# Small zero products on TensorE ahead of the first y burst of a Mamba-2 scan with a SiLU layer

## The chip, the cores and the metric

The kernel runs on one core of one Trainium2 chip. The metric is the device time of one execution in microseconds (us). Six executions of the kernel before are given by their median. One execution was recorded by the hardware profiler; its span, from the first to the last instruction, is shorter than its time, because the start and the end of the execution lie around it.

## The reference, cut to what matters

A chunked state-space scan over 4 batches, 8 heads, 768 positions, head size 32 and state size 16, and after it a layer with SiLU over the 3072 tokens:

```python
for c in range(nc):                       # chunks of 32 positions
    cum = np.cumsum(la, axis=-1)          # la: log of the decays a
    L = np.exp(cum[..., :, None] - cum[..., None, :]) * causal
    M = np.einsum('bhin,bhjn->bhij', Cc, Bc) * L
    y_intra = np.einsum('bhij,bhjd->bhid', M, xc)
    y_inter = np.einsum('bhin,bhnd->bhid', Cc, state) * np.exp(cum)[..., None]
    y[:, :, sl] = y_intra + y_inter
    state = decay_full * state + sum_j(Bc_j xc_j decay_from_j)
...
h = x @ w_in                              # (3072, 256) @ (256, 2048)
g = h * (1.0 / (1.0 + np.exp(-h)))
out = g @ w_out                           # (3072, 2048) @ (2048, 256)
```

## The kernel before

The 3072 tokens are cut into 12 units of 256 positions, three to a batch. The scan uses chunks of 64 positions, four to a unit. The order of the work on each engine is written out by hand; nothing reorders it.

One unit goes through these steps. f_Ab is a TensorE product that spreads the decays of the unit over the partitions (only for units 0 and 1; the others load them spread out); f_Ek or f_E is a scan on DVE (VectorE) that makes the decay factors E from them. f_T (DVE) or f_TP (TensorE transposes, L349) brings B and C into the layout for products, and f_T2 (ACT, which is ScalarE, L359) splits C by even and odd heads into ce. f_B scales B on POOL (L334, tile BT). f_D0 (L383) is a burst of 32 small TensorE records, the chunk states; f_G0 (L398) a burst of 32, C times B. f_S (DVE, L422 and L424) carries the state from chunk to chunk, f_SM (ACT, L432) splits it, f_M (DVE, L409) multiplies f_G0's result by E. f_Y is the y burst: up to 32 records with the state (L452) and 64 with the masked products (L461). f_X (ACT, L470) copies its result to the tile XM. Then f_s1 (L481) multiplies XM by two column blocks of w_in, eight times for a unit, and SiLU follows on ACT. Later the products with w_out follow (L495, and in another form L572).

The weights come in 16 pieces of 512 KB. w_size (ACT) and w_bits (DVE, then POOL at L182) turn each piece into the form that TensorE uses, and w_bits also issues the load of the piece seven further on (L156, SP's queue). Pieces 0 to 2 are issued in the first microseconds, pieces 3 to 6 after the loads of unit 1, and SP issues the loads of unit 2 after them.

The start of the program is a list in one order: transposes and scan of unit 0, y burst of unit 0, first products of unit 0 between the steps of unit 1, y burst of unit 1, and then a table of f_s1 steps with the steps of unit 2 among them.

`busy(n)` issues n products of zeros on TensorE: the tile `idle` is a row of zeros read as bf16, and the result, written to a PSUM tile of the pool ps_o, is read by nobody. It stands at three places: ahead of f_A and the f_Ab of unit 0 (five products, at the start), between f_G0 and f_D0 of unit 0 (four), and between f_Ab of unit 1 and the y burst of unit 0 (four). On TensorE a product is two instructions, a weight load (PEld) and a matmul (PE).

## Time and profile before

| what | value |
|---|---|
| median of 6 executions | 359.45 us |
| all six | 360.4, 357.52, 359.42, 357.7, 359.66, 359.48 us |
| the profiled execution | 360.4 us, span 358.7 us |
| mean granted clock of TensorE over the span | 0.993 |
| TensorE busy | 346.0 us, 96% of the span |
| DVE, ACT, POOL busy | 51%, 45%, 51% |

In the profile's lists a line begins with the start of a group (us from the span's start) and its length, then engine, line of the code, operation, tiles (out<-in), shape and count; in brackets stands how long the engine was idle before the group, and what released it. "issue" there means that the engine waited for nothing that the profile shows. In a table by stretch the columns are the stretch, its length, the busy time and number of instructions of PE, PEld, DVE, ACT and POOL, then the granted clock of TensorE (1.00 is full), the busy share of the 16 DMA engines and GB/s. In the lists of DMA queues stand packets, MB and the share of 16 engines' time; q1 carries the data that SP issues, q8 and q14 carry instructions.

### The profile page before, as it was taken

To read this page: it belongs to the slowest core of one execution; us is meant where nothing else is said; L and a number is where in the kernel's file an instruction comes from. 1 tells how busy PE (TensorE), PEld (TensorE's weight loads), DVE (VectorE), ACT (ScalarE), POOL (GpSimd) and SP (SyncE) were. 2 spreads that over 40 slices of the span, in tenths; PEclk is the share of its full clock that TensorE was granted. 3 is DMA by queue.
4 is the path that set the end of the run, shared out by engine and by line. 5 is a ranking of instruction groups with operands and counts; after the bars stand their busy time and mean duration, and the time that the engine had idled before them with its cause. 6 is when DMAs were issued, how large, how long until landed. Compare 5 with 4: busy or idle time off the path is not lost.

```text
span 358.7 us, 8309 instructions
## 1 busy us (share of the span) xinstructions
PE 346.0 (96%) x3276; PEld 290.0 (81%) x3277; DVE 183.0 (51%) x389; ACT 160.7 (45%) x390; POOL 181.4 (51%) x246
## 2 busy tenths in 40 slices
PE   7778999999999999999999999999999999999994
PEld 2457888888888888888888888888888888888883
DVE  7977979754267245543455543446542221214722
ACT  2547477223222444645444645444645354454100
POOL 4433335353139168298355298355298930596100
PEclk9998999999999999999999999999999999999999
DMA  6898966761547252162126163110000110001203
GB/s 122 201 333 152 335 177 111 137 116 24 117 87 104 55 96 28 33 117 32 15 53 112 27 107 45 17 17 2 15 2 14 18 16 0 15 2 19 40 2 45
DMA packets 110059, 26.53 MB, mean 74 GB/s; under 512 B 98884, under 2 KB 105796, under 8 KB 110020
## 3 DMA queue, kind: packets, MB, share of 16 engines
q1 hardware_dynamic: 107044, 25.67, 35.3%
q10 hardware_dynamic: 2976, 0.33, 0.6%
q8 instruction: 26, 0.43, 0.5%
q14 instruction: 13, 0.11, 0.1%
HBM read 22.83 MB, written 3.15 MB: 72 GB/s over the span
## 4 chain that ended last, share of the span: by engine, by line
PE 91%; SPq 3%; DMA 2%; issue 1%; ACT 1%; DVE 1%; POOL 0%; ACTq 0%; DVEq 0%
PE o_ps L572 30%; PE hp L655 28%; PE hp L481 15%; PE o_ps L495 8%; PE hp L572 3%; PE gy L461 2%; PE gy L452 2%; PE gy L398 2%; SPq L107 1%; DMA tbc<-in_C_dram 1%; PE gy L383 1%; SPq L156 1%; DMA tbc<-in_B_dram 1%; DMA out_dram<-ot 0%; POOL w_in_sb L182 0%
## 5 line engine op out<-in xcount | busy, mean ns | idle before, releaser
L658 DVE TENSOR_TENSOR gT<-hp,p 128x256 f32<-128x256 f32 x64 | 26.9, 421 | 84.6 <-ACT p L669 47.4
L481 PE MATMUL hp<-XM,w_in_sb 128*128 128x256 f32 x256 | 61.0, 389 | 1.5 <-POOL w_in_sb L182 0.8
L661 ACT ACTIVATE gT<-gT 128x256 f32<-128x256 f32 x96 | 39.7, 413 | 42.8 <-DVE gT L658 42.8
L481 PEld LDWEIGHTS hp<-XM,w_in_sb 128*128 128x128 f32 x256 | 49.1, 194 | 9.7 <-POOL w_in_sb L182 1.7
L572 PE MATMUL o_ps<-gT,w_out_sb 128*128 128x256 f32 x224 | 56.5, 379 | 0.0
L334 POOL TENSOR_TENSOR BT<-bn,E 128x256 f32<-128x256 f32 x12 | 8.6, 717 | 94.7 <-PE hp L655 29.7
L655 PE MATMUL hp<-raw 128*128 128x256 f32 x192 | 52.7, 380 | 0.0
L540 POOL TENSOR_TENSOR gT<-gT 128x256 f32<-128x256 f32 x72 | 51.2, 741 | 0.0
L572 PEld LDWEIGHTS o_ps<-gT,w_out_sb 128*128 128x128 f32 x224 | 42.4, 190 | 5.9
L655 PEld LDWEIGHTS hp<-raw 128*128 128x128 f32 x192 | 36.2, 190 | 5.4 <-POOL ps L543 0.6
L483 ACT ACTIVATE gT<-hp 128x512 f32<-128x512 f32 x32 | 19.1, 596 | 41.2 <-PE hp L481 41.2
L669 ACT ACTIVATE p<-hp 128x256 f32<-128x256 f32 x64 | 24.5, 383 | 27.5 <-PE hp L655 25.7
L658 DVE TENSOR_TENSOR gT<-hp,u 128x256 f32<-128x256 f32 x32 | 13.6, 424 | 40.7 <-PE hp L655 40.7
L655 PE MATMUL hp<-XM,w_in_sb 128*128 128x256 f32 x128 | 34.1, 389 | 0.0
L543 POOL TENSOR_TENSOR ps<-ps 128x256 f32<-128x256 f32 x28 | 20.3, 726 | 26.1 <-ACT ps L579 12.8
L495 PE MATMUL o_ps<-w_out_sb,gT 128*128 128x256 f32 x128 | 30.9, 384 | 0.0
L540 POOL TENSOR_TENSOR TN<-gT 128x256 f32<-128x256 f32 x40 | 28.7, 739 | 0.0
L495 PEld LDWEIGHTS o_ps<-w_out_sb,gT 128*128 128x128 f32 x128 | 23.8, 190 | 3.8 <-issue 0.5
L655 PEld LDWEIGHTS hp<-XM,w_in_sb 128*128 128x128 f32 x128 | 23.3, 190 | 4.3 <-issue 1.0
L297 DVE TENSOR_TENSOR_SCAN E<-ab,diag 128x256 f32<-128x256 f32 (+1 forms) x32 | 24.5, 805 | 3.7 <-PE gy L461 3.3
L540 POOL TENSOR_TENSOR gT<-gT,TN 128x256 f32<-128x256 f32 x32 | 22.1, 730 | 0.0
L579 ACT ACTIVATE ps<-o_ps 128x256 f32<-128x256 f32 x31 | 11.9, 383 | 18.5 <-PE o_ps L572 18.2
(121 smaller groups left out, 542.5 us busy)
## 6 DMA issues: line engine op xcount, KB each, us to landing
ab<-in_a_dram SPq DMA_DIRECT2D x40, 128.0 KB, 3.3
raw<-in_moe_w_in_dram SPq DMA_DIRECT2D x8, 512.0 KB, 7.6
raw<-in_moe_w_out_dram SPq DMA_DIRECT2D x8, 512.0 KB, 6.3
xt<-in_x_dram SPq DMA_DIRECT2D x24, 128.0 KB, 4.0
out_dram<-ot SPq DMA_DIRECT2D x76, 32.0 KB, 1.7
bn<-in_B_dram SPq DMA_DIRECT2D x22, 64.0 KB, 4.9
tbc<-in_C_dram SPq DMA_DIRECT2D x40, 32.0 KB, 2.6
pa<-in_a_dram SPq DMA_DIRECT2D x10, 128.0 KB
```

The source lines that it names most:

```text
L297: nc.vector.tensor_tensor_scan(out=E[u].rearrange("p k h t -> p (k h t)")[:, Q * g0:Q * (g0 + n)], data0=t.rearrange("p g t -> p (g t)"), ...
L481: nc.tensor.matmul(out=hp[:, i], lhsT=w_in_sb[:, kc, f * 128:(f + 1) * 128], rhs=xm[:, kc], start=(kc == 0), stop=(kc == KC - 1))
L483: nc.scalar.activation(GTS[g][:, 2 * j:2 * j + 2], hp, AF.Silu)
L495: nc.tensor.matmul(out=o[:, c], lhsT=GTS[g][:, f, 128 * c:128 * c + 128], rhs=w_out_sb[:, f, :], start=(f == 0), stop=(f == NF - 1), skip_ ...
L540: engine.tensor_tensor(out=o[:, j], in0=a0[:, j], in1=a1[:, j], op=ALU.subtract)
L543: engine.tensor_tensor(out=o, in0=p, in1=q, op=ALU.add)
L572: nc.tensor.matmul(out=o, lhsT=w(j), rhs=g()[:, j], start=(j == 0), stop=(j == NF // 2 - 1))
L579: nc.scalar.activation(pn, on, AF.Copy)
L655: nc.tensor.matmul(out=o, lhsT=w, rhs=x_, start=start, stop=True, skip_group_check=True)
L658: nc.vector.tensor_tensor(out=o, in0=p, in1=q, op=ALU.add)
L661: nc.scalar.activation(o, i, AF.Silu)
L669: nc.scalar.activation(o, i, AF.Copy)
```

## The change

`busy` gets a second count: products of 64 columns with 64 rows of the result, the left operand being 64 columns of zeros. One zero product of 512 columns is taken away at two of the three places, and small ones are put at four: 14 at the start, 24 ahead of f_G0 of unit 0 (a new place), 10 between f_G0 and f_D0, and 30 ahead of the y burst of unit 0. An unused argument goes. No other instruction is touched.

```diff
-    def busy(n, early=True):
-        t = ps_o.tile([128, 512], FP32, name="o_ps") if early else ps_s.tile([128, 4, 512], FP32, name="gy")[:, 0]
+    def busy(n, small=0):
+        t = ps_o.tile([128, 512], FP32, name="o_ps")
         for i in range(n):
             nc.tensor.matmul(out=t, lhsT=idle[:, 0:128], rhs=idle, start=True, stop=True)
+        for i in range(small):
+            nc.tensor.matmul(out=t[:64, :64], lhsT=idle[:, 0:64], rhs=idle[:, 64:128], start=True, stop=True)
...
-    busy(5)
+    busy(4, 14)
     f_A()
...
     f_Ab(0, 0)
     f_Ab(0, 1)
+    busy(0, 24)
     f_G0(0)
-    busy(4)
+    busy(4, 10)
     f_Ek(0, 0)
     f_Ek(0, 1)
     f_B(0)
     f_D0(0, True)
...
     f_Ab(1, 0)
     w_size(1)
-    busy(4)
+    busy(3, 30)
     f_Y(0)
     f_Ab(1, 1)
     f_X(0)
```

## The prediction

> **What bounds the kernel now.** I read the page first, then TensorE's timeline over 32 us, then busy time by stretch, then the DMA queues of short windows. From the page:

> ```profile
> span 358.7 us, 8309 instructions
> ...
> PE 346.0 (96%) x3276; PEld 290.0 (81%) x3277; DVE 183.0 (51%) x389; ACT 160.7 (45%) x390; POOL 181.4 (51%) x246
> ...
> PEclk9998999999999999999999999999999999999999
> ...
> q8 instruction: 26, 0.43, 0.5%
> ```

> TensorE is busy 96% of the span, so a microsecond of its idle time taken away early is a microsecond off the end, if nothing else comes late. The clock row has one slice below 9, the fourth. Queue q8 brings instructions: 26 packets, 0.43 MB, so 16.5 KB each; TensorE's 3276 + 3277 records over 26 packets are 252, so a packet is a block of about 256 TensorE instructions. The timeline of TensorE:

> ```profile
> 7.53 0.70 PE L398 MATMUL gy<-ce,bh 32*64 32x128 f32 x32 [1.03 <-ACT ce L359]
> 8.16 1.04 PE L221 MATMUL o_ps<-gT 128*128 128x512 bf16 x4
> 9.52 0.46 PE L383 MATMUL hp<-xt,BT 64*32 64x64 f32 x32 [0.33 <-POOL BT L334]
> 9.91 1.12 PE L305 MATMUL hp<-gT 108*128 108x512 f32 x2
> 10.87 1.03 PE L221 MATMUL o_ps<-gT 128*128 128x512 bf16 x3
> 13.05 0.58 PE L452 MATMUL gy<-cw,sm 32*64 32x64 f32 x24 [1.15 <-DVE E L409]
> 13.56 0.86 PE L461 MATMUL gy<-E,xt 64*32 64x64 f32 x64
> ...
> 18.12 0.33 PE L349 MATMUL o_ps<-ident,tbc 128*128 128x128 f32 x1 [0.51 <-DMA tbc<-in_C_dram]
> ...
> 27.23 0.34 PE L461 MATMUL gy<-E,xt 64*32 64x64 f32 x15 [1.97 <-issue]
> 28.32 4.31 PE L481 MATMUL hp<-XM,w_in_sb 128*128 128x256 f32 x12 [0.74 <-ACT XM L470]
> ```

> The zero products are L221. The longest gap, 1.97 us, lies inside unit 1's y burst, and its releaser is "issue": no engine held it up. From 28.32 on there is no idle time to the last microseconds. By stretch (TensorE busy first, then its weight loads; the granted clock is the number after POOL):

> ```profile
> 22.74:26.15 3.41, 2.52 (x87) 1.90 (x86) 1.95 (x4) 1.60 (x3) 1.26 (x1) 1.00 1.04 378
> 26.15:29.56 3.41, 1.58 (x21) 1.29 (x21) 0.68 (x2) 1.89 (x4) 0.00 (x0) 1.00 1.06 259
> 29.56:32.97 3.41, 3.41 (x10) 2.66 (x9) 3.32 (x6) 2.69 (x5) 1.44 (x2) 0.50 0.52 105
> ...
> ```

> A stretch with 1.58 of 3.41 us busy is followed by exactly one stretch at half clock: 3.41 us of work took twice its time, so 1.71 us were lost. And the queues from 24.8 to 26 us:

> ```profile
> q1 hardware_dynamic: 230, 0.45, 100.6%
> q8 instruction: 1, 0.02, 5.2%
> ```

> One instruction packet falls in the gap: it starts at 24.91, ends at 25.91, and TensorE goes on at 27.23, 2.32 us after its start. I count 704 instructions (345 + 347 in the stretch 0 to 25.27, and 12 semaphore instructions) before the gap: the edge of a block. Edges one block apart lie after instructions 192, 448, 704, 960. The first three q8 packets start at 14.18, 24.91 and 29.41. So I read it thus: crossing an edge asks for the block after the next. The first edge lies in unit 0's y burst (13.05; packet 1.1 us later, among 64-byte packets), the second in D0 of unit 1 (about 20.2; packet 4.7 us later, behind 2 KB packets of the weight pieces), and that block is what the y burst of unit 1 then lacks.

> **The change, part by part.** It removes two zero products of 512 columns and adds 78 of 64 columns. Each product is two instructions, a weight load and a matmul: 76 x 2 = 152 more, 26 of them ahead of Ab, 74 ahead of G0, 94 ahead of D0, all ahead of unit 0's y burst.

> *Their own time.* No row has a 64-column product by itself. In the records the 512-column ones start 0.215 us apart (0.427 before 5.7 us), an eighth of which is 0.027; the f32 128-column transposes (L349) start 0.107 apart. I take 0.048, half the 97 ns weight load of the wide product, and keep 0.027 and 0.107 as ends.
> First place: -0.43 + 14 x 0.096 at the early clock = +0.9 (0.3 to 2.6). It delays the two Ab products, whose scan on DVE starts at 6.38 after the transposes; the first Ab ended at 5.5, so 0.9 us of cover hides it.
> Second: 24 x 0.048 = 1.15 (0.65 to 2.6) in the 1.03 us for which G0 waits on ScalarE: G0 0.2 late. Its only reader, the mask product (L409), comes at 11.62.
> Third: 10 x 0.048 = 0.48 (0.3 to 1.1) between 9.03 and D0's start at 9.52: D0 0.2 late; DVE reads D0 at 10.49 and it ended at 9.98, 0.5 us of cover.
> Fourth: -0.215 + 30 x 0.048 = 1.2 (0.6 to 3.0) in the 1.15 us before the y burst, which waits for DVE: 0.1 us late.
> On the path +0.1, at most +1.7 at the upper ends (D0 2.2 late less its cover of 0.5; DVE is about 95% busy there and passes it on). Nothing is moved on SP's or POOL's queues, and no other engine waits for a zero product.

> *The edges.* With 94 instructions more, edge 192 lies at the third instruction of D0 of unit 0, crossed near 9.2 us. Edge 448 lies in the y burst of unit 0, at its 124th of 176 instructions, near 14.1. Edge 704 lies at the start of unit 1's y burst. The block needed there is now asked for near 14.1 to 16 us, where the DMA engines are less loaded:

> ```profile
> 8.50:12.90 4.40, 3.02 (x41) 1.08 (x39) 4.18 (x10) 1.48 (x4) 1.41 (x2) 1.00 1.00 328
> ...
> 14.20:17.00 2.80, 2.80 (x33) 1.80 (x17) 2.77 (x5) 1.87 (x4) 2.00 (x3) 1.00 0.40 38
> ```

> With the longest delay seen, 4.7, and 2.32 to use, it is there by 23, a microsecond before unit 1's burst at 23.9. So the 1.97 us gap goes, and with it the idle stretch and its half clock: -1.97 - 1.71 = -3.68. The block after that is asked for near 23.8 and there by 31 at the worst; its first instruction ran at 37.6, less 4.

> *What is late next.* The block needed at 14.1 is now asked for at 9.2, amid the weight pieces (8.5 to 12.9 us, 328 GB/s). Its packet starts 1.1 to 4.7 us later; nearest is the row with the weight pieces, but these end at 12.9, so 13 to 13.9, and the rest of unit 0's y burst runs at 15.3 to 16.2: a new gap of 1.2 to 2.1 us (none at the short delay). I take 1.6, resuming at 15.7. It is mostly covered: TensorE waited 0.51 us at 18.12 for the load of C, and 0.80 us at 21.99 for POOL's w_in_sb. Following TensorE from 15.7: y ends at 16.2, XM at 16.9, s1 18.9, transposes 19.3, s1 20.95, D0 0.85 later than before; the state scan on DVE, which began 0.74 after D0, follows, and unit 1's burst starts at 24.15 instead of 23.92. Cost 0.2; at 16.2 it is 0.7.

> *Whether the gain arrives.* DVE waits 4.12 us to 28.85 for ScalarE, which waits for TensorE's y, so DVE moves with the gap, but not with the half clock. G of unit 2 ran at 47.91 and its BT was done at 45.84: 2.07 us of slack against the 1.7 that TensorE gains on DVE. It holds.

> Sum against the profiled execution's 360.4 (span 358.7): 360.4 - 3.68 + 0.1 + 0.2 = 357.0. The profiled run lies 0.95 above the median of 359.45; from the median, 359.45 - 3.4 = 356.1. Two of the six runs, 357.5 and 357.7, are 1.9 faster than the rest, about the price of one half-clock stretch; I read them as runs without it, and 357.6 - 1.97 + 0.3 = 355.9 agrees.

> [...]
> [...]

> **The rivals.** (a) The new gap falls badly in the clock's stretches: 1.6 plus the wait before y is about 2 us of idle time in 3.4. Then 15.9 to 19.3 runs at half clock, +1.7 not covered: 357.8. For it: 1.83 us sufficed above. Against it: the zero products fill the time before, and two of six runs kept the clock even with the longer gap.
> (b) The change does not do what the edges say: another cause than the block holds the burst at 25.27, and the gap stays: 359.5. Against it: the packet in the gap.
> (c) Slower: the block asked for at 9.2 waits behind all that SP has issued by then, as C's load did, which landed at 18.07. Resuming at 20.4, everything up to unit 1's burst shifts to 29, XM to 31, with a half-clock stretch more: +2.7, so 362.1. It decides from a packet later than about 16 us; the longest delay in the trace, 4.7, gives 13.9.

> **How the numbers follow.** A measurement of this kernel can tell about 0.5%, 1.8 us, from no change: faster is below 357.65, slower above 361.25. Forecast (with or without the covered gap, no half clock) 0.70, of 354.9 to 357.2; (a) 0.13, half of it below 357.65; (b) 0.07; (c) 0.10. The lower end, 354.9, is 357.6 less 1.97 and 0.7 of waits in unit 1's stretch that may shrink; the upper, 359.0, takes in (a) with the small products at their upper price. Faster 0.75, same 0.14, slower 0.11.

> **What would show it.** Right: the first q8 packet starts between 10 and 14 us; unit 1's y burst has no "issue" gap; s1 of unit 1 starts near 26.5, not 28.32, and the stretch after it keeps the full clock; any new "issue" gap lies inside unit 0's burst, before 16.5. Wrong: a gap still at 25 us, D0 of unit 0 later than 10.2, unit 1's burst later than 25, or a clock row below 9 between 16 and 20 us.

## The result, and the profile after

The changed kernel takes 357.44 us (median of 36 executions, 356.36 to 360.4); the kernel before, on the same chips, 359.26 us (78 executions, 357.35 to 362.32). The ratio is 0.9964, with a 95% interval of 0.995 to 0.9979: faster by 0.36%, or 1.3 us, where 3.4 us were forecast. The two medians lie 1.8 us apart; the executions fall into two groups of times, so a median can jump between them, and the means of the table below differ by 1.15 us. The profiled execution of the changed kernel took 356.53 us. The first lines of its page and its clock row:

```profile
span 354.8 us, 8461 instructions
...
PE 346.6 (98%) x3352; PEld 291.7 (82%) x3353; DVE 183.4 (52%) x389; ACT 160.5 (45%) x390; POOL 181.7 (51%) x246
...
PEclk9999999999999999999999999999999999999999
```

Against the page of before the span is 3.9 us shorter with the same busy time, and the slice of the clock row below 9 is gone. TensorE's timeline (L223 is the new small product; all lines below it have moved by two):

```profile
7.09 0.94 PE L223 MATMUL o_ps<-gT 128*64 128x64 bf16 x24
7.97 0.69 PE L400 MATMUL gy<-ce,bh 32*64 32x128 f32 x32
8.59 1.04 PE L221 MATMUL o_ps<-gT 128*128 128x512 bf16 x3
9.56 0.50 PE L223 MATMUL o_ps<-gT 128*64 128x64 bf16 x10
9.99 0.45 PE L385 MATMUL hp<-xt,BT 64*32 64x64 f32 x32
...
12.08 1.14 PE L223 MATMUL o_ps<-gT 128*64 128x64 bf16 x30
13.15 0.58 PE L454 MATMUL gy<-cw,sm 32*64 32x64 f32 x24
13.65 0.64 PE L463 MATMUL gy<-E,xt 64*32 64x64 f32 x38
15.34 0.43 PE L463 MATMUL gy<-E,xt 64*32 64x64 f32 x26 [1.04 <-issue]
...
23.96 0.69 PE L454 MATMUL gy<-cw,sm 32*64 32x64 f32 x32
24.58 0.86 PE L463 MATMUL gy<-E,xt 64*32 64x64 f32 x64
26.13 14.08 PE L483 MATMUL hp<-XM,w_in_sb 128*128 128x256 f32 x64 [0.69 <-ACT XM L472]
```

In before the burst of unit 1 was cut after 49 of its 64 masked products:

```profile
24.54 0.73 PE L461 MATMUL gy<-E,xt 64*32 64x64 f32 x49
27.23 0.34 PE L461 MATMUL gy<-E,xt 64*32 64x64 f32 x15 [1.97 <-issue]
```

In after that 1.97 us gap (24.58) is gone, and s1 of unit 1 starts at 26.13 instead of 28.32. A new "issue" gap of 1.04 us lies in unit 0's burst, after 38 of the 64 records of L463. Ahead of it TensorE's records in the trace number 448 (220 products, 222 weight loads and 6 others), ahead of the gap of before 704: 256 apart, one block by the prediction's count. The first q8 packets start at 12.92 and 21.51 (before: 14.18 and 24.91).

So this one execution did what the prediction said, to half a microsecond (360.4 forecast to become 357.0, and 356.53 measured). Over all executions the gain is little more than a third of what was forecast, so that agreement is in part luck, as the section on the prediction shows.

One sum holds in all fourteen profiles, of before, after and the twelve experiments: the time from the first s1 record of unit 1 to the end of the span, less half of the half-clock time that falls into it, is 328.63 to 328.79 us. (Half clock behind TensorE's last product, in the last microseconds, is not taken off: no product is left to slow down.) All that the change does is decided ahead of that record and by the clock.

The executions also list their mean clock. I call 0.996 and more full clock: what is missing then I put down to the stretch at the very end, which is at half clock in both profiles (from 357.24 us in before, from 354.61 in after). Pooled over four sets of before (104 executions) and two of after (49):

| | full clock: share, mean us | lower clock: share, mean us | mean of all |
|---|---|---|---|
| before | 53 of 104, 358.15 | 51 of 104, 359.94 | 359.03 |
| after | 30 of 49, 357.07 | 19 of 49, 359.16 | 357.88 |

One execution of before, 362.8 us, lies far above the rest; without it the lower-clock mean is 359.88 and the mean of all 358.99. At full clock the change is worth 1.08 us, not the 1.67 net that was forecast for the gap; and the half clock, which was to vanish, is there in 39% of the executions instead of 49%.

### The profile page after: what moved, and what is told of

Same layout as the page of the kernel before. It is cut to its first block, busy times and chain, and to the rows that moved or that the text cites. A ratio compares the mean times of both kernels' runs of the same rounds, so it can differ in the third digit from the quotient of the medians.

```text
span 354.8 us, 8461 instructions
## 1 busy us (share of the span) xinstructions
PE 346.6 (98%) x3352; PEld 291.7 (82%) x3353; DVE 183.4 (52%) x389; ACT 160.5 (45%) x390; POOL 181.7 (51%) x246
## 4 chain that ended last, share of the span: by engine, by line
PE 96%; ACT 1%; DVE 1%; issue 1%; DMA 0%; POOL 0%; SPq 0%; DVEq 0%; ACTq 0%
PE o_ps L574 30%; PE hp L657 28%; PE hp L483 15%; PE o_ps L497 8%; PE hp L574 3%; PE gy L463 3%; PE gy L454 2%; PE gy L400 2%; PE hp L307 1%; PE gy L385 1%; PE o_ps L221 1%; PE o_ps L223 1%; DMA out_dram<-ot 0%; POOL w_in_sb L182 0%; SPq L554 0%
## 5 line engine op out<-in xcount | busy, mean ns | idle before, releaser
L483 PE MATMUL hp<-XM,w_in_sb 128*128 128x256 f32 x256 | 59.3, 381 | 1.0 <-ACT XM L472 0.7
L483 PEld LDWEIGHTS hp<-XM,w_in_sb 128*128 128x128 f32 x256 | 48.1, 190 | 8.5 <-POOL w_in_sb L182 1.1
L657 PE MATMUL hp<-XM,w_in_sb 128*128 128x256 f32 x128 | 34.1, 389 | 0.0
L497 PEld LDWEIGHTS o_ps<-w_out_sb,gT 128*128 128x128 f32 x128 | 23.8, 190 | 3.8 <-issue 0.5
L657 PEld LDWEIGHTS hp<-XM,w_in_sb 128*128 128x128 f32 x128 | 23.3, 190 | 4.3 <-issue 1.0
L581 ACT ACTIVATE ps<-o_ps 128x256 f32<-128x256 f32 x31 | 11.9, 384 | 18.5 <-PE o_ps L574 18.2
```

Of the source, the lines that this page charges most:

```text
L483: nc.tensor.matmul(out=hp[:, i], lhsT=w_in_sb[:, kc, f * 128:(f + 1) * 128], rhs=xm[:, kc], start=(kc == 0), stop=(kc == KC - 1))
L497: nc.tensor.matmul(out=o[:, c], lhsT=GTS[g][:, f, 128 * c:128 * c + 128], rhs=w_out_sb[:, f, :], start=(f == 0), stop=(f == NF - 1), skip_ ...
L581: nc.scalar.activation(pn, on, AF.Copy)
L657: nc.tensor.matmul(out=o, lhsT=w, rhs=x_, start=start, stop=True, skip_group_check=True)
```

## Experiments: which part does it

Each edit is shown against the changed kernel, and each ratio is to the kernel before, run in the same set.

**The first two places alone**, `busy(4)` left as it was at the other two:

```diff
-    busy(4, 10)
+    busy(4)
...
-    busy(3, 30)
+    busy(4)
```

> Only the first two places of the change (14 and 24 small products, one wide one less): 74 instructions more, all ahead of f_G0 of unit 0. Edge theory (a block of 256 TensorE instructions that arrives late makes the gap): the edge that lay in unit 0's y burst now lies in the transposes of unit 1 near 17 us, and its block, asked for near 9.5 us, is usable near 15.4; so no issue gap in either y burst, s1 of unit 1 starts at 25.8 to 26.2 us, and the median is 356.3 to 357.0, below the 357.44 of the whole change, with fewer runs at a reduced clock. Rival (the zero work just ahead of the y burst is what helps, by keeping TensorE active): with the third and fourth place as before, the gap near 25 us stays and the median is 358.5 to 359.5.

**The last two places alone**:

```diff
-    busy(4, 14)
+    busy(5)
...
-    busy(0, 24)
```

> Only the last two places of the change (10 and 30 small products, one wide one less): 78 instructions more, between f_G0 of unit 0 and its y burst. Edge theory: the second edge lies at the end of the first s1 of unit 0 near 16.9 us; its block is asked for near 10.5 us, behind the weight pieces, and is usable at 15.3 to 16.2: no gap in either y burst, s1 of unit 1 at 25.8 to 26.3, median 356.3 to 357.2. Rival (the zero work matters by its place and activity): a result between before and after, 358 to 359, and different from the first two places alone.

**Wide products of the same length instead**:

```diff
-    busy(4, 14)
+    busy(6)
...
-    busy(0, 24)
+    busy(4)
...
-    busy(4, 10)
+    busy(6)
...
-    busy(3, 30)
+    busy(8)
```

> Zero work of the same length as after at the same four places, but of wide products alone (6, 4, 6 and 8): only 22 instructions more than before. Edge theory: the gap stays in unit 1's y burst, eleven products earlier, 1.5 to 2.2 us long, none in unit 0's burst; median 358.9 to 359.6, the same as before. Rival (activity): the gap or the half-clock stretch after it goes, median 356.5 to 358.

Medians (12 executions each) and ratios to the kernel before: first two 356.87 us, 0.9943 (0.9919 to 0.9968); last two 357.05, 0.9952 (0.9933 to 0.9972); wide instead 359.67, 1.0014 (0.9989 to 1.0039). At a lower clock were 2, 2 and 9 of 12. Either half of the small products brings as much as the whole change or more, at quite different places; the same zero work in few instructions brings nothing. In the timeline of the wide kernel, and then of the first two places alone:

```profile
24.92 0.64 PE L463 MATMUL gy<-E,xt 64*32 64x64 f32 x38
27.35 0.60 PE L463 MATMUL gy<-E,xt 64*32 64x64 f32 x26 [1.79 <-issue]
28.65 11.68 PE L483 MATMUL hp<-XM,w_in_sb 128*128 128x256 f32 x40 [0.70 <-ACT XM L472]
```

```profile
24.98 0.75 PE L463 MATMUL gy<-E,xt 64*32 64x64 f32 x52 [0.19 <-issue]
26.41 13.86 PE L483 MATMUL hp<-XM,w_in_sb 128*128 128x256 f32 x63 [0.69 <-ACT XM L472]
```

With 22 more instructions the gap is still in unit 1's burst, after 38 records instead of 49: eleven products earlier, as the block edge demands. With 74 or 78 it is 0.19 us or none. So the gap follows the place of the block edge, and TensorE's activity as such does not take it away. (What activity does to the clock is another question, below.) Two things missed: the wide kernel's median lies 0.07 us above its forecast, and s1 of unit 1 started at 26.41 and 26.58 in the two half changes, not by 26.2 and 26.3. In these two profiles TensorE waited 0.95 and 0.94 us for POOL's w_in_sb ahead of the third s1 of unit 0, more than the 0.29 of after.

**Before again**, unedited, for a second profile:

> The kernel before without an edit, for a second profile. Edge theory: again an issue gap after the 49th record of unit 1's masked products, from a packet that starts 4 to 5 us after D0 of unit 1. The remainder from s1 of unit 1 to the end is 328.66 us plus 1.71 for each stretch at half clock, in all profiles so far; so a run at 358.3 without half clock must have s1 of unit 1 at 27.9, not 28.32.

```profile
25.08 0.73 PE L461 MATMUL gy<-E,xt 64*32 64x64 f32 x49
28.41 0.46 PE L461 MATMUL gy<-E,xt 64*32 64x64 f32 x15 [2.61 <-issue]
29.62 10.74 PE L481 MATMUL hp<-XM,w_in_sb 128*128 128x256 f32 x37 [0.75 <-ACT XM L470]
```

The gap is at the same record, 2.61 us long this time, from a packet that started at 25.99, 5.3 us after its edge was crossed at 20.69 (4 to 5 were expected). It was one execution of 362.51 us, with two half-clock stretches; the remainder was 328.63. For the full-clock executions of before, 358.15 less the 1.73 around the span and 328.65 puts s1 of unit 1 at 27.8. That is an estimate; by it the gap is shorter there than in either profile, if the waits ahead of it are alike.

## Experiments: where the half clock comes from

**After again**, unedited:

> The changed kernel without an edit, for the spread of its runs and their clocks beside the other kernels. If the half-clock stretches follow the gap in unit 0's y burst, about a third of the runs show a mean clock of 0.988 to 0.995 and take 1.5 to 3.5 us more than the rest; median 357.0 to 357.8. If they have another cause, the kernels without any gap show them as often.

Median 357.80 us, 6 of 12 at a lower clock (a third was expected; the two half changes, without a gap in this burst, had 2 of 12 each), and the profile fell on one of those (358.75 us). Its stretches, then its timeline:

```profile
9.19:12.60 3.41, 3.33 (x68) 1.94 (x68) 3.19 (x8) 0.85 (x3) 1.29 (x2) 1.00 1.01 358
12.60:16.02 3.42, 1.93 (x104) 1.59 (x100) 3.35 (x8) 2.07 (x4) 1.31 (x2) 1.00 0.71 134
16.02:19.43 3.41, 3.41 (x23) 2.04 (x7) 3.30 (x4) 1.72 (x3) 1.66 (x2) 0.50 1.01 134
```

```profile
15.72 0.45 PE L463 MATMUL gy<-E,xt 64*32 64x64 f32 x26 [1.19 <-issue]
28.23 12.14 PE L483 MATMUL hp<-XM,w_in_sb 128*128 128x256 f32 x55 [0.69 <-ACT XM L472]
```

The gap in unit 0's burst is 1.19 us here and lies in one clock stretch with the wait ahead of the burst: 1.93 of 3.42 us busy, then a stretch at 0.50, and s1 of unit 1 at 28.23 instead of 26.13. In the first profile of after the stretch from 13.28 to 16.69 had 2.37 us busy and the clock stayed. The stretches begin at another time in every profile, 5.15 us (the first two places alone) to 10.81 (before again) for the first that the clock records show, so it is a matter of luck which idle times fall together.

**All waits filled, no edge in unit 0's burst**, with the first two places as in the change:

```diff
-    busy(4, 10)
+    busy(6)
...
-    busy(3, 30)
+    busy(8)
```

> The first two places as in the change (4 and 14, 24), and in the third and fourth wide products alone (6 and 8): 86 instructions more than before, so no edge in a y burst, and every wait of TensorE ahead of unit 0's y burst filled. If a stretch of 3.41 us goes to half clock when TensorE is busy for less than about 2 us of the one ahead of it (1.92 did, 2.37 did not), and if the late blocks and the empty waits are the only such stretches, hardly any run (0 or 1 of 12) has a clock below 0.996, all lie at 356.4 to 357.6, median 356.8, mean 0.3 to 0.5 below the two half changes (357.33 and 357.18). Rival (the half-clock stretches come from elsewhere, or by chance): 2 to 5 of 12 runs at a low clock, as in the half changes and the full one.

**One wait emptied**, the last place with nothing:

```diff
-    busy(4, 10)
+    busy(4)
...
-    busy(3, 30)
```

> The first two places as in the change, four wide products in the third, none in the fourth: 66 instructions more than before, no edge in a y burst and so no issue gap, but TensorE stands idle for about 2.1 us ahead of unit 0's y burst. If idle time in a clock stretch makes the half clock whatever its cause, half or more of the runs show 0.988 to 0.995 and take 1.5 to 3.5 us more than the rest; the others lie at 356.4 to 357.6; median 357.5 to 359.5. Rival (only a gap for instructions does it): as the first two places alone, median 356.9, 2 of 12 at a low clock.

Filled: 1 of 12 at a lower clock, median 357.27 us, 0.9957 (0.9934 to 0.998). Emptied: 9 of 12, median 357.66, 0.9975 (0.9952 to 0.9999). A gap for instructions is not needed to lower the clock: the emptied kernel has no issue gap, only the wait for DVE (1.76 us, to 13.31), and its stretches read

```profile
10.85:14.26 3.41, 1.65 (x69) 0.91 (x70) 3.19 (x9) 2.57 (x6) 0.68 (x1) 1.00 1.05 251
14.26:17.68 3.42, 3.42 (x40) 2.04 (x35) 3.39 (x5) 2.04 (x4) 2.41 (x3) 0.50 0.68 78
```

Two expectations missed. The emptied kernel's lower-clock executions averaged 358.01 us against 357.13 for the other three: 0.9 us, not 1.5 to 3.5, for a half clock that ends at 17.68 in the profile. Six of the nine list a mean clock of 0.987, by an estimate from the 0.995 of the profiled execution more than one such stretch, and four of those six still took only 357.55 to 357.92. The waits of TensorE at 18 and 22 us, seen in before, can take it up; this is argued, not tried. The same stretch two microseconds later, in after again, put s1 of unit 1 2.1 us later than in the first profile of after. And the filled kernel was slower than its forecast by 0.5, for it has a gap again, in the other burst:

```profile
24.54 0.31 PE L463 MATMUL gy<-E,xt 64*32 64x64 f32 x6
26.04 0.80 PE L463 MATMUL gy<-E,xt 64*32 64x64 f32 x58 [1.19 <-issue]
```

Its third edge lies at the sixth record there, and the packet that it waits for started at 23.59, 7.4 us after TensorE crossed the second edge at 16.20, where by the reading in the prediction it was asked for. I had argued for after that a block asked for near 15 us is there early. In after it took 6.2 us (15.34 to 21.51) and came, by the 2.32 us from packet to use in before, 0.2 us ahead of its need.

**The edge behind or inside unit 0's burst**, eight products apart and with equal zero work:

```diff
-    busy(4, 10)
+    busy(4, 6)
...
-    busy(3, 30)
+    busy(8)          # behind; busy(7, 9) puts the edge inside
```

> The first two places as in the change, then 4 wide and 6 small, then 8 wide: 94 instructions more than before, so that the second edge falls right behind unit 0's y burst and the first Ab behind it (in s1 of unit 0), with every wait ahead of the burst filled. Theory (the gap inside unit 0's burst puts a clock stretch below the limit of about 2 us busy, and that half clock is what the change loses): no issue gap in unit 0's burst, at most 0.7 us of idle time behind it; 0 to 2 of 12 runs below a clock of 0.996; median 356.5 to 357.2. Rival (the half clock comes with the start, whatever the edges): 4 to 6 of 12 at a low clock, median 357.2 to 358.2.

> The same with one wide product less and 9 small ones more in the last place: 110 instructions more than before, and the second edge five products ahead of the end of unit 0's y burst; the zero work takes as long within 0.1 us. Theory: an issue gap of 0.8 to 1.3 us inside unit 0's burst; 4 to 6 of 12 runs at a low clock, 1 to 2.5 us longer; full-clock runs as in the kernel with the edge behind the burst within 0.3; median 357.2 to 358.0. Rival: no difference between the two.

Behind: median 356.89 us, 0.9949 (0.992 to 0.9977), 1 of 12 at a lower clock. Inside: 357.76, 0.9978 (0.9951 to 1.0005), 4 of 12. The profiled execution with the edge inside:

```profile
15.37 0.31 PE L463 MATMUL gy<-E,xt 64*32 64x64 f32 x5 [0.84 <-issue]
...
26.00 14.08 PE L483 MATMUL hp<-XM,w_in_sb 128*128 128x256 f32 x64 [0.69 <-ACT XM L472]
```

It has the gap, 0.84 us, and yet s1 of unit 1 at 26.00, earlier than the 26.68 in the profile with the edge behind, as this execution, the fastest of its twelve, kept its clock. So in this execution the gap in unit 0's burst by itself was covered, as forecast; what it costs then is the chance of a half clock. Over the executions that is less clear. Those at full clock average 357.40 with the edge inside and 356.95 with it behind, 0.45 apart where at most 0.3 was expected, while after, with a gap in the same burst, averages 357.07. Whether a part of the gap is left uncovered stays open. Four against one of twelve is a thin difference taken alone; with the filled and the emptied kernel (1 and 9) and after (19 of 49) it is of one kind.

## Experiments: what makes a block late, and a better version

**The loads of unit 1 ahead of weight pieces 0 to 2** (in after):

```diff
-    for n in range(3):
-        load_w(n, nc.sync)
     load_n(1, 0, nc.sync)
     load_n(1, 1, nc.sync)
     load_x(1, nc.sync)
+    for n in range(3):
+        load_w(n, nc.sync)
```

> The changed kernel with the loads of unit 1 (64 and 128-byte packets) issued ahead of the weight pieces 0 to 2 (2 KB packets), so that the block asked for near 9 us meets small packets. If the 2 KB packets queued ahead of it make an instruction packet late, the first q8 packet starts near 10 to 11 us instead of 12.9 and there is no issue gap in unit 0's y burst; the time is not the point, since the pieces arrive some 4 us later and s1 of unit 0 waits for them. Rival (a block takes 4 us at that point of the program whatever else is queued): first packet at 12.5 to 13.5 and the gap of about 1 us stays.

One execution, 362.12 us, with the first packet at 10.83 and no gap in the burst, as the theory had it: with 1493 packets under 512 bytes on the data queue from 10.7 to 12 us, the block came 0.3 us after its edge (10.58). The price is a wait of 3.84 us for the weights ahead of the first s1.

**Piece 2 alone moved** behind B and C of unit 1 (in after):

```diff
-    for n in range(3):
+    for n in range(2):
         load_w(n, nc.sync)
     load_n(1, 0, nc.sync)
     load_n(1, 1, nc.sync)
+    load_w(2, nc.sync)
     load_x(1, nc.sync)
```

> The changed kernel with weight piece 2 issued behind B and C of unit 1: fewer 2 KB packets are queued when the block for unit 0's burst is asked for. Theory: first q8 packet at 11.3 to 11.9 us (two pieces less one third of the wait), no issue gap in unit 0's burst, 0 to 2 of 12 runs below 0.996, median 356.3 to 357.0, ahead of the changed kernel and of the kernel before. Rival (the packet takes its time whatever is queued, or piece 2 then comes late for POOL): gap as in after, or TensorE waits more than 0.8 us for w_in_sb near 22 us; median 357.3 or more.

Median 356.83 us, 0.9948 (0.9924 to 0.9972), 1 of 12 at a lower clock: the time is as the theory had it. The profile is not. It fell on that one lower-clock execution (358.83 us), whose first packet started at 13.53, not 11.3 to 11.9, with a gap of

```profile
16.10 0.43 PE L464 MATMUL gy<-E,xt 64*32 64x64 f32 x26 [1.59 <-issue]
```

So in this execution the wait of the packet did not follow from the number of 2 KB packets ahead of it. The first edge lies in D0 of unit 0 in after and in these two runs, and the packet started 2.9 us after it in after (10.00 to 12.92), 0.3 in the run before this one (10.58 to 10.83) and 3.5 here (10.06, the start of D0, to 13.53). What sets it stays open.

**Both together**, the edge behind the burst and piece 2 moved:

> The edge right behind unit 0's y burst (94 instructions more than before) and piece 2 issued behind B and C of unit 1. Theory (late blocks and the half clock that follows them are what is left to gain): no issue gap in either y burst, 0 or 1 of 12 runs below a clock of 0.996, median 356.4 to 356.9, mean below 357.0, about 2 us below the kernel before and 0.6 to 0.9 below the changed one. Rival (what is left is the chain of VectorE and POOL, and the two edits take away the same thing): median 356.7 to 357.0, no better than either alone; if piece 2 comes late for POOL, more than 0.95 us of idle time ahead of the third s1 of unit 0 and a median over 357.2.

Median 357.02 us (356.56 to 357.48), 0.9938 (0.9918 to 0.9958), none of 12 below 0.996; the median is 0.1 above the theory's range. Its mean, 357.01, is 0.9 below that of after and 2.0 below that of before, and its slowest execution took 357.48. But at full clock it is no faster than after (357.07): the rival's reading. Its profile has 0.62 us of issue gap left in unit 1's burst and 0.82 us of waiting for w_in_sb. Piece 2 alone has the best mean, 356.96; the two can't be told apart. Both are better than before and, by the means, than the changed kernel.

## Why the prediction was right and wrong

Right: the edges. The place of the new gap, after 38 records of the masked products, the start of the first packet (10 to 14; 12.92), the end of the gap (15.3 to 16.2; 15.34), s1 of unit 1 (near 26.5; 26.13), unit 1's burst without a gap, and, in the profiles, that the new gap by itself is covered (over the executions this stays open). The small products were cheaper than taken: 0.032 us apart from 7 us on and 0.053 at 3 us, against 0.048 and 0.096; unit 0's burst started 0.1 late, as forecast (13.15 against 13.05; 13.38 in after again). Not all on the way there was right: edge 192 was crossed at 10.0 and not near 9.2, for D0 of unit 0 started at 9.99, 0.47 late where 0.2 was forecast, and with 0.2 it could not have been crossed before 9.7. Rival (b) fell; so did rival (c): the gap in unit 0's burst ended at 15.34 in after and at 15.72 in after again, not at 20.4. That the gain passes to the end holds to 0.16 us (328.63 to 328.79).

The edges cost time: TensorE stopped at them for 1.97 us in before and for 1.04 in after, and the same zero work with and without the added instructions differs by 1.9 us in the median (359.67 against 357.80, in the same set). And idle time in pieces was followed by half clock: in after again a gap of 1.19 us with 0.30 us of waiting beside it.

Wrong: the size, at two terms of the sum.

First, the half clock, -1.71: the step "the 1.97 us gap goes, and with it the idle stretch and its half clock". The sum took it off the median in full, as if every execution of before had it and none of after. By the clocks of the executions 49% of before have it, at 1.79 us more than the rest, and 39% of after, at 2.09: 0.88 against 0.81 us in the mean. The term was worth -0.07. In the profiles that show it, the half clock was not removed but moved, from behind unit 1's burst to behind unit 0's. This is rival (a), given 0.13 as an all-or-nothing case (the 1.83 us it names are 3.41 less the 1.58 us busy of the stretch from 26.15 in before); it comes at the place forecast (16.02 to 19.43; 15.9 to 19.3 forecast) and at a little more than the price forecast (2.1 us against 1.7). Two of the six executions shown before the prediction were read as free of it, and that should have led to a mean over executions and not to a median that has it.

Second, the gap, -1.97 with 0.3 given back. At full clock the difference is 1.08. The profile of before was a late one (s1 of unit 1 at 28.32, where the full-clock mean asks for 27.8), and that of after an early one (26.13 against 26.7 by the same sum): an estimate, which puts the rest of the difference down to which executions were profiled. Less of a gap brings little more: five kernels with no edge in unit 0's burst (the two half changes, waits filled, edge behind, both together) average 357.02 at full clock over 54 executions, though their profiles show from none to 1.19 us of the gap in unit 1's burst. In four of these five profiles the wait for w_in_sb ahead of unit 1's burst, 0.82 to 0.95 us, is the longest one left between the two bursts. That it now sets the time was not tried.

The two together give -1.15, and the means of the pooled executions differ by that. The range held the time, the sign was right, and the chance of 0.75 for a gain over 0.5%, where the ratio gives 0.36%, rests on a sum into which the spread between executions entered with no term.

## What to carry to other kernels

Where an engine stops with "issue" inside a dense burst of small instructions, count its instructions against its instruction packets: if the stops sit at one spacing (here 256, from 448 in after to 704 in before), the place of an instruction in the stream is a cost of its own, and some harmless instructions ahead can move the edge out of the burst (94 did in the run with the edge behind the burst, whose profile has no issue gap in either y burst). Place the edge, don't only move it: look where every following edge then falls and how long ahead its block is asked for. And before a cost read from one profile is taken off a median, ask in what share of the executions it is there; a list of clocks beside the times tells it.
